# Gated linear attention with one routed token: spinning on zeros at the start, a router argmax in two levels, four q features inside the end of K, and the last attention tile turned by DMA

## The chip, the cores and the metric

The kernel runs on one core of a Trainium2 chip, in one launch. The metric is the device time of an execution in microseconds (us), the median of several runs. TensorE is called PE here, its weight loads PEld, VectorE DVE, ScalarE ACT, GpSimd POOL and SyncE SP, as in the profile. "Lnn" is line nn of the kernel before; where a line of the changed kernel is meant, the text says so.

## The reference

Three results are mixed: a linear attention `a`, a layer `b` that changes a single token, and a gate `g` per token.

```
x = A_x                                             # (1, 2048, 1024), bf16
g = sigmoid((x * gate_w).sum(-1))                   # one gate per token
q, k, v = split(x @ wqkv)                           # 32 heads of 32
phi(u) = concat(softmax(u @ w_phi), softmax(-(u @ w_phi)))   # 64 features per head
kv = sum_s phi(k)_s v_s ;  z = sum_s phi(k)_s
a = (phi(q) @ kv / (phi(q) @ z + 1e-6)) @ wo
r = x @ w_r ;  idx = argmax(r)                      # one token out of 2048
y = (silu(x[idx] @ w_gate) * (x[idx] @ w_up)) @ w_down * sigmoid(r[idx])
b = x, with y added to row idx                      # w_gate, w_up: 1024 x 3584
out = g * a + (1 - g) * b
```

## The kernel before, in words

A scheduler puts the program's instructions in order on each engine and sets the semaphores; the order in the code and the buffers of the pools decide what it can do. Each engine then works through its own list in that order. The 2048 tokens are 16 tiles of 128. There are three stages.

**V (to about 74 us).** Four tiles of x are loaded (`xs_t`, L247) and transposed on PE (`xT_tile`, L269, copied by DVE, L270); the other twelve come by transposing DMAs (L273), all issued on SP. `k_v` (L392) multiplies each tile with the value weights in three pieces of 256, 384 and 386 columns; the last two columns are the router's and the gate's weight rows, put there by `rows_in` (L260). `fold` (L287) multiplies the key and query weights with `w_phi` once, so that keys and queries give features directly; it needs sixteen transposed weight loads (`wT`, six buffers, L279).

**K (about 74 to 161 us).** 32 units: one tile and half the heads each. `k_s0` makes the feature inputs `pk` (L405, eight matmuls with 512 columns), ACT takes exp of plus and minus (`e`, L408 and L409, three buffers), DVE sums and inverts (`ssum` L412, `rs` L414), and the product `phi` (L417) is made on POOL, every fourth one on DVE. `k_kv` adds phi times v into PSUM (`kvps`, L426) five units later (`LAG`).

At the start of K stands the router, `gates_and_route` (L293). `r` is transposed to 16 rows of 128 (`rT`, L304), a DMA strings them into one row (`r_row`, L306), and DVE finds the maximum (L308) and its place (L310) among 2048 values on one partition. The place is read into registers of DVE and POOL, DVE copies the token's column out of `xT` (`xsT`, L313), and PE multiplies it with the gate's row (`gw_sel`, L315). A short chain over ACT, DVE and PE (`ee`, `cc`, `c_bc`) makes one factor of it.

The chosen token's layer runs beside K and Q in 21 chunks of 1 MB of weights (`ffn_chunk`, L352 and L369; pool `ring` with two buffers): each chunk is 32 narrow matmuls with `xsT` or, for `w_down`, with `hh`.

**Q (about 161 to 304 us).** `kv_finish` copies the sums out of PSUM into `KV` (L446, L448, L449), DVE and ACT in turns. Then one loop runs over 32 steps and some more: `q_front` (L463) makes 512 tokens of features for four heads, ACT writes their exponentials to `E` (L465, L466); four steps later `q_num` (L484) multiplies with KV, DVE scales (`T`, L492), POOL adds and divides (`U` L501, `o_sb` L502); a transposing DMA turns the tile (`oT`, L511), ACT scales x (`xg`, L521, four buffers), and `q_wo` multiplies with `wo` (`po`, L530) in two groups of eight matmuls per tile, some steps later (`WL`). DVE mixes (`o_out`, L533) and SP stores (L539). The last tile is not turned by a DMA but by eight transposes on PE (`oT_ps`, L515) and an ACT copy. At the end POOL adds `y` into the chosen row (L384), behind all stores.

PSUM pools matter for order: `psA` (two buffers) serves pv, pk and pq; `psB` (two) serves pT, pW, po and `oT_ps`; `psK` has one buffer for kvps or num; everything small, the router's products among them, shares one tile, `small_ps`.

Of the kernel before, what the change touches and what calls it, by code (L numbers as in the profile page):

```python
# [20 lines left out]
D = 1024  # L21
H = 32
DH = 32
NT = S // P
KB = D // P
# [4 lines left out]
NU = NT * 2  # L30
# [7 lines left out]
VW = 1026  # L38
TX = 4
# [126 lines left out]
def kernel(  # L166
# [14 lines left out]
    ring = main.enter_context(tc.tile_pool(name="ring", bufs=2))  # L181
# [9 lines left out]
    wk = kscope.enter_context(tc.tile_pool(name="wk", bufs=3))  # L191

# [48 lines left out]

    xtiles = {}
# [7 lines left out]
    wv_sb = wraw.tile([P, KB, VW], BF, name="wv_sb", tag="w16")  # L250
# [42 lines left out]
    def gates_and_route():  # L293
# [11 lines left out]
        r_row = const.tile([1, S], BF, name="r_row")  # L305
        nc.sync.dma_start(out=r_row[0:1, :], in_=rT[:])  # L306
        mx8 = const.tile([1, 8], F32, name="mx8")
        nc.vector.max(out=mx8[:], in_=r_row[:])  # L308
        ix8 = const.tile([1, 8], U32, name="ix8")
        nc.vector.max_index(out=ix8[:], in_max=mx8[:], in_values=r_row[:])  # L310
        idx_dve = nc.values_load(ix8[0:1, 0:1], engines=[ET.DVE], min_val=0, max_val=S - 1)
        moe["idx_pool"] = nc.values_load(ix8[0:1, 0:1], engines=[ET.Pool], min_val=0, max_val=S - 1)
# [5 lines left out]
        nc.scalar.activation(out=ee[:, 0:1], in_=mx8[0:1, 0:1], func=ACTF.Exp, scale=-1.0)  # L318
# [138 lines left out]
    def q_front(sb, j):  # L457
        if j == 0:
            est[sb] = qp["eb"].tile([P, KB, 2, SB], BF, name="E", tag="E")
        E = est[sb]  # L460
        pq = psA.tile([P, SB], F32, name="pq", tag="pA")
        for kb in range(KB):
            nc.tensor.matmul(pq[:], lhsT=wqf[:, kb, j * P:(j + 1) * P], rhs=xT[:, kb, sb * SB:(sb + 1) * SB],  # L463
                             start=(kb == 0), stop=(kb == KB - 1))
        nc.scalar.activation(out=E[:, j, 0, :], in_=pq[:], func=ACTF.Exp)  # L465
        nc.scalar.activation(out=E[:, j, 1, :], in_=pq[:], func=ACTF.Exp, scale=-1.0)  # L466

    def q_num(t, hf):
# [3 lines left out]
        if hf == 0:  # L472
            st = {"o": qw.tile([P, H, DH], BF, name="o_sb", tag="o_sb", bufs=5)}
            xin = qw.tile([P, D], BF, name="xin", tag="xin", bufs=8)
# [30 lines left out]
    def q_oT(t):  # L505
# [4 lines left out]
        if t < NT - 1:  # L510
            nc.sync.dma_start_transpose(out=oT[:], in_=o_f)  # L511
        else:
            oT_ps = psB.tile([P, KB, P], BF, name="oT_ps", tag="pB")
            for kb in range(KB):
                nc.tensor.transpose(out=oT_ps[:, kb, :], in_=o_f[:, kb * P:(kb + 1) * P], identity=ident[:])  # L515
            nc.scalar.copy(out=oT[:], in_=oT_ps[:])
# [31 lines left out]

    xT_tile(0)
    rows_in()  # L550
    k_v(0, 0)
# [36 lines left out]
    qp["eb"] = main.enter_context(tc.tile_pool(name="eb", bufs=2))  # L588
# [4 lines left out]
    WL = 6  # L593
    wq_ = []
    i = 0
    while i < n_front + NL + 2 or wq_:
# [11 lines left out]
        if i < n_front:  # L608
            q_front(i // KB, i % KB)
# [43 lines left out]
```

## Time and profile before

| what | before |
|---|---|
| median of 3 runs | 306.57 us (305.55 to 307.3) |
| the profiled execution's own time | 305.89 us |
| its span, first to last instruction | 304.2 us |
| granted TensorE clock, mean | 0.990 |
| PE busy | 278.5 us, 2483 matmuls |
| DVE busy | 185.0 us |
| ACT busy | 145.4 us |
| POOL busy | 126.1 us |
| DMA | 47.45 MB, 156 GB/s on average |

The profile shows one execution. A row of a timeline reads: start, duration, engine, line, operation, written tile, read tiles, shapes, how many were merged, and in brackets the idle time of the engine before the first with what ended it. A row of the waits reads: who waits, for whom, us in total, how often, the longest. A row of the windows gives a stretch, then for each engine the busy time and the count, then the granted clock, the share of DMA time and GB/s.

### The profile page before, as it was taken

What the parts mean: (1) busy time and instruction counts of PE and PEld (TensorE: products, weight loads), DVE (VectorE), ACT (ScalarE), POOL (GpSimd) and SP (SyncE); (2) the same over time, 40 slices, a digit from 0 to 9 for tenths busy, and PEclk for the clock granted to TensorE, in tenths of its full rate; (3) what the DMA queues carried; (4) which work ended last, traced back from release to release, by engine and by line L of the source; (5) the groups of instructions that cost most, each with busy time, mean ns of one, the idle gap of its engine ahead of it and who ended that gap; (6) DMA issues with size and microseconds to landing.
All of it is one profiled execution on the core that took longest, in us unless ns stands there. A gap on an engine that the chain in (4) does not pass through costs nothing. (4 is left out here: it accounts for less than half of the span.)

```text
span 304.2 us, 6228 instructions
## 1 busy us (share of the span) xinstructions
PE 278.5 (92%) x2483; PEld 163.7 (54%) x2518; DVE 185.0 (61%) x362; ACT 145.4 (48%) x266; POOL 126.1 (41%) x105
## 2 busy tenths in 40 slices
PE   2999999999898799999979999999999999996990
PEld 2756667766345456656545556555555555552440
DVE  3200015466899777778794677777668666694340
ACT  1133345877744343544427999465555443422100
POOL 6000000000166555755560588865556666674001
PEclk9999999999999999999999999999999999997998
DMA  7999999960001897766745989814542242134220
GB/s 205 283 178 186 197 336 294 150 122 0 1 2 29 269 313 240 260 203 213 254 168 183 313 326 258 168 38 104 131 111 71 52 106 69 34 94 98 69 87 25
DMA packets 76529, 47.45 MB, mean 156 GB/s; under 512 B 47824, under 2 KB 69328, under 8 KB 76496
## 3 DMA queue, kind: packets, MB, share of 16 engines
q1 hardware_dynamic: 75344, 46.94, 57.8%
q8 instruction: 21, 0.34, 0.5%
q10 hardware_dynamic: 1120, 0.07, 0.3%
q14 instruction: 12, 0.10, 0.1%
q0 software_dynamic: 32, 0.00, 0.0%
HBM read 31.53 MB, written 4.20 MB: 117 GB/s over the span
## 5 line engine op out<-in xcount | busy, mean ns | idle before, releaser
L417 POOL TENSOR_TENSOR phi<-e,rs 128x1024 bf16<-128x1024 bf16 x24 | 45.7, 1912 | 106.1 <-DVE rs L414 97.8
L405 PE MATMUL pk<-wkf,xT 128*128 128x512 bf16 x240 | 59.9, 379 | 2.9 <-ACT e L409 1.9
L530 PE MATMUL po<-wo_sb,oT 128*128 128x512 bf16 x249 | 59.7, 384 | 2.3 <-DVE o_out L533 1.7
L392 PE MATMUL pv<-wv_sb,xT 128*128 128x256 bf16 (+2 forms) x384 | 61.1, 313 | 0.3 <-DVE xT L270 0.3
L463 PE MATMUL pq<-xT,wqf 128*128 128x512 bf16 x244 | 60.5, 379 | 0.8 <-ACT E L466 0.2
L501 POOL TENSOR_TENSOR U<-T 128x512 f32<-128x512 f32 x32 | 40.6, 1268 | 43.1 <-DVE T L492 27.0
L392 PEld LDWEIGHTS <-xT 128*128 128x128 bf16 x384 | 37.1, 99 | 18.3 <-DVE xT L270 0.5
L412 DVE TENSOR_REDUCE ssum<-e 128x32 f32<-128x1024 bf16 x32 | 38.6, 1211 | 11.8 <-ACT e L409 11.8
L533 DVE SCALAR_TENSOR_TENSOR o_out<-po,gate,xg 128x512 bf16<-128x512 f32 x32 | 24.0, 750 | 32.1 <-PE po L530 32.0
L530 PEld LDWEIGHTS <-oT 128*128 128x128 bf16 x256 | 25.1, 99 | 31.0 <-issue 3.0
L408 ACT ACTIVATE e<-pk 128x512 bf16<-128x512 f32 x32 | 19.1, 597 | 41.6 <-PE pk L405 26.7
L492 DVE TENSOR_TENSOR T<-num,rS 128x1024 f32<-128x1024 f32 x32 | 38.9, 1215 | 0.0
L394 ACT CAST v_all<-pv 128x384 bf16<-128x384 f32 (+1 forms) x48 | 21.2, 444 | 34.7 <-PE pv L392 34.4
L405 PEld LDWEIGHTS <-xT 128*128 128x128 bf16 x256 | 22.8, 97 | 24.0 <-issue 2.3
L463 PEld LDWEIGHTS <-wqf 128*128 128x128 bf16 x256 | 23.4, 98 | 21.8 <-issue 0.3
L502 POOL TENSOR_TENSOR o_sb<-U,rden 128x512 bf16<-128x512 f32 x32 | 33.6, 1049 | 2.5
L521 ACT ACTIVATE xg<-xin,omg 128x1024 f32<-128x1024 bf16 x16 | 18.4, 1151 | 23.4 <-DVE o_out L533 23.4
L465 ACT ACTIVATE E<-pq 128x512 bf16<-128x512 f32 x32 | 19.1, 596 | 19.5 <-PE pq L463 19.3
L519 ACT ACTIVATE junk<-xin 128x1024 bf16<-128x1024 bf16 x16 | 17.0, 1062 | 11.6 <-DMA xin<-in_A_x_dram 11.5
L484 PEld LDWEIGHTS <-E 128*128 128x128 bf16 x256 | 17.0, 98 | 9.0 <-DVE T L492 2.6
L484 PE MATMUL num<-KV,E 128*128 128x136 bf16 x256 | 20.8, 223 | 0.2 <-DVE KV L449 0.2
L466 ACT ACTIVATE E<-pq 128x512 bf16<-128x512 f32 x32 | 19.0, 595 | 0.0
(95 smaller groups left out, 243.6 us busy)
## 6 DMA issues: line engine op xcount, KB each, us to landing
wch<-in_B_w_gate_dram SPq DMA_DIRECT2D x7, 1024.0 KB, 6.7
wch<-in_B_w_up_dram SPq DMA_DIRECT2D x7, 1024.0 KB, 5.1
wchd<-in_B_w_down_dram SPq DMA_DIRECT2D x7, 1024.0 KB, 5.8
xin<-in_A_x_dram SPq DMA_DIRECT2D x16, 256.0 KB, 4.1
out_dram<-o_out SPq DMA_DIRECT2D x32, 128.0 KB, 1.8
wo_sb<-in_A_wo_dram SPq DMA_DIRECT2D x1, 2048.0 KB, 13.8
wv_sb<-in_A_wqkv_dram SPq DMA_DIRECT2D x2, 768.0 KB, 8.2
xs_t<-in_A_x_dram SPq DMA_DIRECT2D x4, 256.0 KB, 4.5
```

The costliest lines, as they stand in the source:

```text
L392: nc.tensor.matmul(pv[:, 0:hi - lo], lhsT=xT[:, kb, t * P:(t + 1) * P], rhs=wv_sb[:, kb, lo:hi], start=(kb == 0), stop=(kb == KB - 1))
L394: nc.scalar.copy(out=v_all[:, t, h0:h1, 0:DH], in_=pv[:, 0:(h1 - h0) * DH].rearrange("p (h d) -> p h d", d=DH))
L405: nc.tensor.matmul(pkf, lhsT=xT[:, kb, t * P:(t + 1) * P], rhs=wkf[:, kb, hf * 512:(hf + 1) * 512], start=(kb == 0), stop=(kb == KB - 1))
L412: nc.vector.tensor_reduce(out=ssum[:], in_=e2, axis=AX.X, op=ALU.add)
L417: eng.tensor_tensor(out=phi[:].rearrange("p h s f -> p (h s) f"), in0=e2, in1=_bc(rs[:], [P, HH * 2, DH]), op=ALU.mult)
L463: nc.tensor.matmul(pq[:], lhsT=wqf[:, kb, j * P:(j + 1) * P], rhs=xT[:, kb, sb * SB:(sb + 1) * SB], start=(kb == 0), stop=(kb == KB - 1))
L484: nc.tensor.matmul(num[:, b * NSTR:b * NSTR + KVW], lhsT=E[:, j, sg, tl * P:(tl + 1) * P], rhs=KV[:, sg, j, :], start=True, stop=True)
L492: nc.vector.tensor_tensor(out=T[:].rearrange("p s (j h) d -> p (s j) h d", h=4), in0=nb[:, :, 0:128].rearrange("p b (h d) -> p b h d", d=D ...
L501: nc.gpsimd.tensor_tensor(out=U[:], in0=T[:, 0], in1=T[:, 1], op=ALU.add)
L502: nc.gpsimd.tensor_tensor(out=st["o"][:, hf * HH:(hf + 1) * HH, :], in0=U[:], in1=_bc(rden[:], [P, HH, DH]), op=ALU.mult)
L530: nc.tensor.matmul(po[:], lhsT=st["oT"][:, kb, :], rhs=wo_sb[:, kb, sl], start=(kb == 0), stop=(kb == KB - 1))
L533: nc.vector.scalar_tensor_tensor(out=o_out[:], in0=po[:], scalar=gate[:, t:t + 1], in1=st["xg"][:, sl], op0=ALU.mult, op1=ALU.add)
```

## The change

Five edits stand together.

1. A tile of zeros, `wz`, is written as DVE's first work. Seven 512-wide matmuls on it are issued before everything else on PE, and three more after `rows_in` in the code. They write `small_ps`, which nobody reads then.
2. The argmax goes in two levels. DVE finds the maximum and its place in each of the 16 rows of `rT`, adds the row's offset (`row0`, an iota on POOL), and a DMA brings the 16 pairs to one partition (`mrow`). There DVE takes the largest value, puts a large number on the place of every row that is below it (`cnd`), takes the smallest place (`ixf`) and casts it (`ixi`).
3. The pool `ring` of weight chunks has three buffers. The room of `wv_sb` (`w16`) becomes a pool of its own that `E` uses in turn with one buffer of `eb`; `xin` has seven buffers in place of eight.
4. The first four `q_front` (`NPRE`) are called inside the last steps of the K loop.
5. The last tile is turned by a transposing DMA like the others, and `WL` is 8 in place of 6, so that each `q_wo` comes two steps later.

```diff
+NPRE = 4
-    ring = main.enter_context(tc.tile_pool(name="ring", bufs=2))
+    w16 = main.enter_context(tc.tile_pool(name="w16", bufs=1))
+    ring = main.enter_context(tc.tile_pool(name="ring", bufs=3))
...
+    wz = const.tile([P, 512], BF, name="wz")
+    nc.vector.memset(wz[:], 0.0)
+
+    def spin(n):
+        for _ in range(n):
+            nc.tensor.matmul(small_ps[:, 0:512], lhsT=wz[:, 0:P], rhs=wz[:], start=True, stop=True)
...
+    nc.gpsimd.iota(row0[:], pattern=[[0, 1]], base=0, channel_multiplier=P, allow_small_or_imprecise_dtypes=True)
...
-        nc.sync.dma_start(out=r_row[0:1, :], in_=rT[:])
-        mx8 = const.tile([1, 8], F32, name="mx8")
-        nc.vector.max(out=mx8[:], in_=r_row[:])
-        nc.vector.max_index(out=ix8[:], in_max=mx8[:], in_values=r_row[:])
-        idx_dve = nc.values_load(ix8[0:1, 0:1], engines=[ET.DVE], min_val=0, max_val=S - 1)
+        nc.vector.max(out=mx8[:], in_=rT[:])
+        nc.vector.max_index(out=ix8[:], in_max=mx8[:], in_values=rT[:])
+        nc.vector.tensor_copy(out=mi[:, 0:1], in_=mx8[:, 0:1])
+        nc.vector.tensor_copy(out=mi[:, 1:2], in_=ix8[:, 0:1])
+        nc.vector.tensor_tensor(out=mi[:, 1:2], in0=mi[:, 1:2], in1=row0[:], op=ALU.add)
+        nc.sync.dma_start(out=mrow[0:1, :, :], in_=mi[:])
+        nc.vector.tensor_reduce(out=mxv[:], in_=mrow[:, :, 0], axis=AX.X, op=ALU.max)
+        nc.vector.tensor_scalar(out=cnd[:], in0=mrow[:, :, 0], scalar1=mxv[:, 0:1], scalar2=float(2 * S),
+                                op0=ALU.is_lt, op1=ALU.mult)
+        nc.vector.tensor_tensor(out=cnd[:], in0=cnd[:], in1=mrow[:, :, 1], op=ALU.add)
+        nc.vector.tensor_reduce(out=ixf[:], in_=cnd[:], axis=AX.X, op=ALU.min)
+        nc.vector.tensor_copy(out=ixi[:], in_=ixf[:])
+        idx_dve = nc.values_load(ixi[0:1, 0:1], engines=[ET.DVE], min_val=0, max_val=S - 1)
...
-            est[sb] = qp["eb"].tile([P, KB, 2, SB], BF, name="E", tag="E")
+            ep = w16 if sb % 2 == 0 else qp["eb"]
+            est[sb] = ep.tile([P, KB, 2, SB], BF, name="E", tag="w16" if sb % 2 == 0 else "E")
...
-        if t < NT - 1:
-            nc.sync.dma_start_transpose(out=oT[:], in_=o_f)
-        else:
-            oT_ps = psB.tile([P, KB, P], BF, name="oT_ps", tag="pB")
-            for kb in range(KB):
-                nc.tensor.transpose(out=oT_ps[:, kb, :], in_=o_f[:, kb * P:(kb + 1) * P], identity=ident[:])
-            nc.scalar.copy(out=oT[:], in_=oT_ps[:])
+        nc.sync.dma_start_transpose(out=oT[:], in_=o_f)
...
+    spin(7)
     xT_tile(0)
     rows_in()
+    spin(3)
     k_v(0, 0)
...
+        if i >= NU and i - NU < NPRE:
+            q_front(0, i - NU)
...
-    WL = 6
+    WL = 8
...
-        if i < n_front:
+        if NPRE <= i < n_front:
             q_front(i // KB, i % KB)
```

What that does to the order shows best at three places. The first is DVE at the start of K, where `ssum` and `rs` belong to the K units and the rest to the router. Before:

```order
L412 TENSOR_REDUCE ssum<-e 128x32 x2
L414 RECIPROCAL rs<-ssum 128x32 x2
L412 TENSOR_REDUCE ssum<-e 128x32
L308 MAX mx_961<-r_row 1x8
L414 RECIPROCAL rs<-ssum 128x32
L310 MAX_INDEX ix_963<-mx_961,r_row 1x8
L412 TENSOR_REDUCE ssum<-e 128x32
L311 TENSOR_LOAD ix_963
...
L313 COPY xsT<-xT 128x8
```

The same place in the changed kernel (its lines), from the arrival of the 16 pairs on:

```order
L437 TENSOR_REDUCE ssum<-e 128x32 x2
L327 TENSOR_REDUCE mxv<-mrow 1x1
L439 RECIPROCAL rs<-ssum 128x32
L329 TENSOR_SCALAR cnd<-mrow,mxv 1x16
L439 RECIPROCAL rs<-ssum 128x32
L331 TENSOR_TENSOR cnd<-cnd,mrow 1x16
L437 TENSOR_REDUCE ssum<-e 128x32
L333 TENSOR_REDUCE ixf<-cnd 1x1
L439 RECIPROCAL rs<-ssum 128x32
L335 CAST ixi<-ixf 1x1
L336 TENSOR_LOAD ixi
...
L338 COPY xsT<-xT 128x8
```

The merge lies between the sums of the first three units, and no sum stands between the cast and the register load any more, as one did between L310 and L311.

The second place is PE at the start of K. The numbers tell buffers apart; each row stands for a run of like matmuls and their weight loads. Before:

```order
L405 MATMUL pk_1076<-wkf_112,xT_109 128x512
...
L426 MATMUL kvps_126<-v_all_113,phi_1020 128x66
...
L405 MATMUL pk_1136<-wkf_112,xT_109 128x512
...
L426 MATMUL kvps_126<-v_all_113,phi_1038 128x66
...
L405 MATMUL pk_1162<-wkf_112,xT_109 128x512
...
L426 MATMUL kvps_126<-v_all_113,phi_1056 128x66
...
L405 MATMUL pk_1222<-wkf_112,xT_109 128x512
...
L315 MATMUL small_ps_125<-gw_sel_122,xsT_121 1x1
```

And in the changed kernel, from the same fifth pk tile on:

```order
L430 MATMUL pk_1106<-wkf_117,xT_114 128x512
...
L340 MATMUL small_ps_130<-gw_sel_127,xsT_126 1x1
...
L451 MATMUL kvps_131<-v_all_118,phi_1050 128x66
...
L430 MATMUL pk_1166<-wkf_117,xT_114 128x512
...
L451 MATMUL kvps_131<-v_all_118,phi_1068 128x66
...
L430 MATMUL pk_1192<-wkf_117,xT_114 128x512
L349 MATMUL small_ps_130<-cc_1029,ones_row_101 128x1
```

The product of `gw_sel` with `xsT`, which stood behind three kv groups and most of three pk tiles, now stands directly behind the fifth pk tile.

The third place is the end of PE's list, behind the last num. Before:

```order
L530 MATMUL po_4042<-wo_sb_111,oT_3673 128x512
...
L515 MATMUL oT_ps_4055<-ident_91,o_sb_3852 128x128
...
L334 MATMUL small_ps_125<-nbb_4072,ones_col_98 1x2
...
L530 MATMUL po_4081<-wo_sb_111,oT_3727 128x512
...
L515 MATMUL oT_ps_4055<-ident_91,o_sb_3852 128x128
...
L530 MATMUL po_4081<-wo_sb_111,oT_3727 128x512
```

In the changed kernel:

```order
L550 MATMUL po_4048<-wo_sb_116,oT_3628 128x512
...
L359 MATMUL small_ps_130<-nbb_4069,ones_col_103 1x2
...
L550 MATMUL po_4078<-wo_sb_116,oT_3679 128x512
...
L550 MATMUL po_4090<-wo_sb_116,oT_3679 128x512
...
L550 MATMUL po_4102<-wo_sb_116,oT_3733 128x512
```

The eight transposes are gone. Of the 256 po matmuls 98 stand behind the last num, where before it was 82. Further up, 32 pq matmuls have moved in among the last five kv groups of K, and between the last kv group and the first num of Q stand 96 chunk and 19 pq matmuls, where before it was 64 and 21.

More of the change, by code (lines that the diff above doesn't have):

```diff
@@ L240, in kv_slot @@
         return kvps[:, pr * KSTR:pr * KSTR + 66]
+    row0 = const.tile([NT, 1], F32, name="row0")
+    nc.gpsimd.iota(row0[:], pattern=[[0, 1]], base=0, channel_multiplier=P, allow_small_or_imprecise_dtypes=True)
     xtiles = {}
@@ L248, in xload @@
         xtiles[t] = xt_
-    wv_sb = wraw.tile([P, KB, VW], BF, name="wv_sb", tag="w16")
+    wv_sb = w16.tile([P, KB, VW], BF, name="wv_sb", tag="w16")
     xload(0)
@@ L473, in q_num @@
             st = {"o": qw.tile([P, H, DH], BF, name="o_sb", tag="o_sb", bufs=5)}
-            xin = qw.tile([P, D], BF, name="xin", tag="xin", bufs=8)
+            xin = qw.tile([P, D], BF, name="xin", tag="xin", bufs=7)
             nc.sync.dma_start(out=xin[:], in_=x2[t * P:(t + 1) * P, :])
```

16 lines of the change are left out of this document (11 added, 5 removed).

## The prediction

> **What bounds the kernel now.** I read the page's busy times first, then the waits of TensorE (PE), then the windows and timelines around each wait.
>
> ```profile
> PE 278.5 (92%) x2483; PEld 163.7 (54%) x2518; DVE 185.0 (61%) x362; ACT 145.4 (48%) x266; POOL 126.1 (41%) x105
> ...
> PE pT L269 <- DMA xs_t<-in_A_x_dram: 5.5, 2, 3.8
> PE small_ps L356 <- DMA wch<-in_B_w_gate_dram: 2.1, 2, 1.8
> PE pk L405 <- ACT e L409: 1.9, 3, 1.0
> PE po L530 <- DVE o_out L533: 1.7, 1, 1.7
> PE kvps L426 <- POOL phi L417: 1.5, 1, 1.5
> PE kvps L426 <- DVE phi L417: 1.3, 2, 0.8
> ```
>
> PE is the bound: 278.5 of the 304.2 us span. The rest is the start, the end after the last matmul, and the waits above, which come at stage borders. The change must win there, or where PE runs on half its clock.
>
> ```profile
> 40.00:60.00 20.00, 20.00 (x170) 13.92 (x169) 9.01 (x18) 12.84 (x28) 0.00 (x0) 1.00 1.09 263
> 80.00:100.00 20.00, 18.02 (x185) 9.93 (x187) 19.07 (x27) 8.91 (x19) 11.39 (x6) 1.00 0.11 33
> ...
> 277.80:281.10 3.30, 3.08 (x11) 1.21 (x11) 0.87 (x2) 1.01 (x1) 0.00 (x0) 0.50 0.01 3
> ...
> 285.00:297.00 12.00, 11.25 (x52) 4.91 (x51) 5.23 (x8) 0.00 (x0) 0.00 (x0) 1.00 0.23 78
> ```
>
> After the times come busy us (and count) of PE, PEld, DVE, ACT, POOL, then the granted clock. In the V stage (40 to 60) PE never waits. At the start of K (80 to 100) it idles 1.98 us, and DVE is full (19.07 of 20). From 277.8 to 281.1 the clock is 0.50. The last row gives the full-clock pace of 512-wide matmuls: 11.25 / 52 = 0.216 us.
>
> **The start.**
>
> ```profile
> 5.62 0.33 SPq L247 DMA_DIRECT2D xs_t<-in_A_x_dram  x1
> ...
> xs_t<-in_A_x_dram SPq DMA_DIRECT2D x1, 256.0 KB, 6.1
> ...
> 6.85 1.04 PE L269 MATMUL pT<-ident,xs_t 128*128 128x128 bf16 x8 [1.67 <-DMA xs_t<-in_A_x_dram]
> 7.68 3.62 PE L392 MATMUL pv<-wv_sb,xT 128*128 128x256 bf16 x16
> 11.09 1.30 PE L269 MATMUL pT<-ident,xs_t 128*128 128x128 bf16 x16
> 12.68 0.50 PE L392 MATMUL pv<-wv_sb,xT 128*128 128x256 bf16 x3 [0.29 <-DVE xT L270]
> 13.24 0.93 PE L392 MATMUL pv<-wv_sb,xT 128*128 128x256 bf16 x7
> ```
>
> Sixteen matmuls start between 7.68 and 11.09: 0.213 us each. Later seven take 0.93, about 0.11 each once the last one's latency is off. So PE is on half clock until about 11. The eight transposes at 6.85 take 0.83 until the next matmul; at full clock 0.43. The change spins seven 512-wide matmuls before the first transposes (3.0 us at half clock, estimated at twice 0.216 each; the memset of `wz` is DVE's first work, so they run from about 1.3 to 4.3. That pushes the transposes at 3.79 back by 0.5, which the 1.67 of waiting before 6.85 hides; without that wait it would cost the 0.5) and three more before the second value matmul. If PE is fast from 6.85, it would be through the 16 by 6.85 + 0.43 + 0.65 + 1.73 = 9.7. But then the fourth x tile is late: issued at 5.62, it lands 6.1 us later, at 11.7. Its transposes end near 12.2, where 12.68 stood: **-0.5**, not the 2 us that the clock alone suggests. If PE is still slow, three spins of 0.43 sit on the path, partly taken up by the wait at 11.7: +0.4 to +0.8.
>
> The Trainium skill ("TensorE: Matmul & The Clock Gate", Part 1) says that full clock comes after one busy window of 3413 ns, and that the windows run free of the kernel. By it, 3 us of spin followed by a gap wakes PE only in some executions, and the sum below would be about 1 us higher in the others.
>
> **The router at the start of K.** The argmax over 2,048 values on one partition becomes 16 rows of 128, then a merge of 16 pairs.
>
> ```profile
> 79.78 5.34 PE L405 MATMUL pk<-wkf,xT 128*128 128x512 bf16 x23 [1.04 <-ACT e L409]
> 82.03 0.55 DVE L414 RECIPROCAL rs<-ssum 128x32 f32<-128x32 f32 x2
> 82.55 3.78 POOL L417 TENSOR_TENSOR phi<-e,rs 128x1024 bf16<-128x1024 bf16 x2 [76.43 <-DVE rs L414]
> 83.96 2.27 DVE L308 MAX8 mx<-r_row 1x8 f32<-1x2048 bf16 x1
> 86.44 2.27 DVE L310 FIND_INDEX8 ix<-mx,r_row 1x8 uint32<-1x2048 bf16 x1
> 90.05 0.17 DVE L313 COPY xsT<-xT 128x8 bf16 x1 [0.23 <-DVE ssum L412]
> 90.45 0.34 PE L315 MATMUL small_ps<-gw_sel,xsT 128*1 128x1 bf16 x8
> ...
> r_row<-rT SPq DMA_DIRECT2D x1, 4.0 KB, 1.8
> ```
>
> Two DVE passes of 2.27 go: 4.5 us off DVE. About ten small operations of 0.1 to 0.3 come (like the 0.17 and 0.09 of `xsT` and, below, `cc`); POOL's iota is done long before. The new DMA (`mrow`) is issued near 79.6 and, taking 1.8 like `r_row`, lands at 81.4, before DVE is free at 82.1. But the order also moves the eight `gw_sel` matmuls: they stand right behind the fifth pk tile, ahead of every kv matmul. PE gets there at 79.78 + 5.34 = 85.1 and stops until `xsT` is there. Queued behind the stop are kv group 0, whose phi is ready at 84.5, and the next pk tile; ACT's exponentials wait for that tile, and DVE's sums for them. So the index now has a due time, 85, where before PE had 5.4 us more of other work ahead of it (`gw_sel` at 90.45).
>
> When does it come? From the index to `xsT` the register load takes 90.05 - 88.71 = 1.34 us; before, a reduction covered it, now nothing does. And the merge falls into POOL's phi products, 82.55 to 88.5. These rows show what DVE does beside POOL:
>
> ```profile
> 92.99 0.09 DVE L323 TENSOR_TENSOR cc<-ee 1x1 bf16<-1x1 f32 x1
> ...
> 153.65 1.91 POOL L417 TENSOR_TENSOR phi<-e,rs 128x1024 bf16<-128x1024 bf16 x1 [0.28 <-ACT sg L360]
> 154.63 0.96 DVE L361 TENSOR_SCALAR sg<-sg 128x28 f32<-128x28 f32 x1
> ...
> 275.21 1.27 POOL L501 TENSOR_TENSOR U<-T 128x512 f32<-128x512 f32 x1 [0.23 <-DVE T L492]
> 276.28 0.21 DVE L340 TENSOR_TENSOR bb<-bb 1x1 f32<-1x1 f32 x1
> ```
>
> 28 elements take 0.96 us and end at 155.59, just behind POOL's 155.56. One element takes 0.21 and ends at 276.49, just behind POOL's 276.48; with POOL idle its like took 0.09. So some DVE operations wait out POOL's. Before, the two long passes ran beside POOL at full speed, and the rest of the chain met an idle POOL. In the new chain the add of `cnd` and `mrow` (two SBUF inputs, as L340) is such a one. I work it through: rs ends 82.45, phi(0) holds until 84.6, add 84.7, reduction of 1.2 to 85.9, minimum, rs and cast to 86.6, register 1.34, `xsT` 88.0 to 88.6, `gw_sel` near **88.6**. PE idles 3.5, then 0.4 more for `cc`, against the 1.9 that go: +2.1. A stop that long should also halve the clock, as the row at 277.80 shows after a stretch with 1.73 and 0.70 of waits: 3.4 us at half clock is 1.7, less the 0.4 then hidden: +1.3. Together **+3.4**. Bounds: nothing blocked, `gw_sel` at 86.4, -0.6; a second phi before the add, `gw_sel` at 90.6, +5.8.
>
> The Trainium skill ("SBUF — State Buffer", Who interferes with whom) says that copies and casts within SBUF can need the same port pair. No row here shows the cast or the `xsT` copy under POOL; by the page `gw_sel` is at 88.9 and the sum 0.3 higher.
>
> **The weight chunks.**
>
> ```profile
> 103.68 0.95 PE L356 MATMUL small_ps<-xsT,wch 128*128 128x1 bf16 x32 [1.79 <-DMA wch<-in_B_w_gate_dram]
> ```
>
> The third chunk was late by 1.79, a later one by 0.3. With three buffers it is loaded before K: **-2.1** (from -1.5). Its megabyte now goes ahead of `wo_sb` and ten key weight loads: 4 us at the 263 GB/s of the row at 40. PE does not wait there now, so part of 4 us may show; with the smaller drifts of the Q stage (`WL` 8, 7 `xin` buffers) I take **+0.4** (0 to +1.5).
>
> **From K to Q.**
>
> ```profile
> 157.98 0.43 PE L426 MATMUL kvps<-v_all,phi 128*128 128x66 bf16 x8 [1.51 <-POOL phi L417]
> ...
> 160.79 0.43 PE L426 MATMUL kvps<-v_all,phi 128*128 128x66 bf16 x8 [0.43 <-DVE phi L417]
> ...
> 167.51 0.35 PE L484 MATMUL num<-KV,E 128*128 128x136 bf16 x3 [0.16 <-DVE KV L449]
> ```
>
> Four q tiles (4 x 1.73 us, eight matmuls each) now lie between the last five kv groups; the last phi is there long before. 1.51 + 0.43 go, and about the 0.16. The tiles' exponentials (E) go into the room of `wv_sb`, which the V stage has long left, so ACT need not wait for the K stage's memory; eight of them stand before the KV casts in ACT's order, but the last is done within 1.2 us of its tile, about when the last kv ends. Next late is KV: 6.3 us from the last kv to its last copy (161.2 to 167.5). PE then has 96 chunk matmuls (three chunks at 0.9) and 19 q matmuls (4.1): 6.8 us, which covers it. **-2.0** (from -1.2).
>
> **The tail.**
>
> ```profile
> 273.22 0.59 PE L530 MATMUL po<-wo_sb,oT 128*128 128x512 bf16 x2
> ...
> 275.94 1.02 PE L530 MATMUL po<-wo_sb,oT 128*128 128x512 bf16 x4 [1.73 <-DVE o_out L533]
> 277.66 0.58 PE L515 MATMUL oT_ps<-ident,o_sb 128*128 128x128 bf16 x4 [0.70 <-POOL o_sb L502]
> 280.09 16.21 PE L530 MATMUL po<-wo_sb,oT 128*128 128x512 bf16 x71
> ...
> 275.14 0.74 DVE L533 SCALAR_TENSOR_TENSOR o_out<-po,gate,xg 128x512 bf16<-128x512 f32 x1
> ```
>
> Behind the last num stand 82 po matmuls: 17.7 us at 0.216, 18.4 with the few small ones. They took 273.22 to 296.30, 23.1: 4.7 lost to the waits, to eight transposes and to half clock. `oT_ps` held one of the two psB buffers that po needs. Now 98 po follow without transposes (16 of them were done earlier before, so no PE work is added). One wait stays: the second group after the last num needs the buffer that the `o_out` at 275.14 frees at 275.9, and PE is there at 275.4 (273.65 and one group of 1.73), so about 0.6 with the start. The last tile is turned by a DMA on SP's queue, with only output stores behind it; its product is the last of the 12 groups, 19 us later, so its few us are hidden. Were that cover gone, they would be bare. No wait is left that could halve the clock. **-4.1** (-3.3 to -4.7).
>
> **Sum.** -0.5 + 3.4 - 2.1 + 0.4 - 2.0 - 4.1 = -4.9. The profiled execution took 305.89 us (span 304.2 and 1.7 around it): **301.0**. It lies 0.7 under the median of 306.57; from that the sum gives 301.7.
>
> **Rivals.**
> - The router is quick: no blocking, `gw_sel` at 86.4, -0.6 for +3.4: 297.0. For it: POOL's start trails rs by 0.2. Against it: L340.
> - POOL's second phi goes ahead of the waiting add: 90.6, +5.8: 303.4. No row shows who goes first when both wait.
> - The spin does not wake PE (+0.8 for -0.5): 302.3.
> - Slower: four operations of the chain (`cnd`, add, cast, `xsT`) each wait out a phi of 1.91. `gw_sel` at 93.3: a stop of 8.2 for 1.9, and two halved stretches of 1.7: +9.8, in all 307.4. It decides from `gw_sel` at about 92. Against it: only three phi are ready then.
>
> **How the numbers follow.** Forecast 0.45, quick router 0.24, second phi 0.17, no waking 0.07, slower 0.07. The range 296.2 to 304.0 takes in the first four with their bounds and leaves half of the quick cases' lower tail and the slower case out. A measurement tells about 0.5% (1.5 us): faster 0.89, within 0.07, slower 0.04.
>
> **What would show it.** Right: at the start, a PE wait for the fourth x tile's DMA ahead of its transposes, near 10 to 11.7; PE waiting for DVE `xsT` for 3 to 4 us near 85, with a 0.50 clock behind it; the add of `cnd` as long as what is left of POOL's phi; no wait on `wch`; no wait on phi at the end of K; some 98 po after the last num with one wait. Wrong: `gw_sel` after a wait of under 2 us (the quick router), a half clock after the spins' end (no waking), waits of the folds on `wT`, or po waits in the tail of more than 1 us.

## The result, and the profile after

| | before | changed |
|---|---|---|
| time, median of 4 runs | 306.94 us (305.55 to 308.44) | 296.65 us (295.86 to 297.04) |
| ratio | | 0.966, 95% interval 0.961 to 0.971 |
| profiled execution | 305.89 us, span 304.2 | 297.04 us, span 295.3 |

The changed kernel is 3.4% faster. The forecast was 301.0 with a range of 296.2 to 304.0: the sign is right, the time lies just inside, and the point is 4.3 us too high. By the medians the change is worth 10.3 us (8.9 between the two profiled executions), twice the 4.9 of the forecast. It came out where the quick-router rival (297.0) had put it. Ratios, here and below, leave disturbed runs out; medians and ranges are of all runs.

The first part of the page and the PE waits of the changed kernel, to be laid beside those of before:

```profile
PE 278.5 (94%) x2487; PEld 162.6 (55%) x2520; DVE 181.9 (62%) x371; ACT 143.5 (49%) x265; POOL 126.1 (43%) x106
...
PE pT L280 <- DMA xs_t<-in_A_x_dram: 2.1, 2, 1.2
PE small_ps L340 <- DVE xsT L338: 1.4, 1, 1.4
PE small_ps L200 <- DVE wz L196: 1.3, 1, 1.3
PE pk L430 <- ACT e L434: 1.0, 1, 1.0
PE small_ps L271 <- DMA rows<-in_gate_w_dram: 0.7, 1, 0.7
PE small_ps L349 <- DVE cc L348: 0.4, 1, 0.4
```

PE is busy 278.5 us in both, ten spins among them now; the 8.9 us came out of its idle time and its half clock. The waits for `wch`, for the last phi and for `o_out` are gone. New are the stop for `xsT`, 1.35 us, and 0.42 for `cc`. That is the first surprise: the forecast had a stop of 3.5 there, with a half clock behind it.

Where the time came from, by the two traces: the first pk starts at 74.74 instead of 73.90 (+0.84). From there to the end of the last po it took 222.40 us before (73.90 to 296.30) and 212.47 after (74.74 to 287.21): -9.93. What follows the last po grew by 0.16.

PE's timeline at the start, and the clock in two of its windows (time, busy us and count of PE, PEld, DVE, ACT, POOL, then the granted clock):

```profile
1.35 3.15 PE L200 MATMUL small_ps<-wz 128*128 128x512 bf16 x7 [1.35 <-DVE wz L196]
4.31 0.64 PE L280 MATMUL pT<-ident,xs_t 128*128 128x128 bf16 x8
5.61 0.16 PE L271 MATMUL small_ps<-ident,rows 16*128 16x16 bf16 x1 [0.67 <-DMA rows<-in_gate_w_dram]
6.94 0.62 PE L280 MATMUL pT<-ident,xs_t 128*128 128x128 bf16 x8 [1.16 <-DMA xs_t<-in_A_x_dram]
...
8.52 3.10 PE L417 MATMUL pv<-wv_sb,xT 128*128 128x256 bf16 x15
...
12.98 0.62 PE L280 MATMUL pT<-ident,xs_t 128*128 128x128 bf16 x8 [0.92 <-DMA xs_t<-in_A_x_dram]
```
```profile
7.76:11.17 3.41, 3.41 (x16) 2.06 (x15) 0.53 (x1) 0.38 (x1) 0.00 (x0) 0.50 1.05 346
4.35:7.76 3.41, 1.58 (x21) 1.21 (x20) 1.10 (x4) 1.06 (x1) 1.67 (x10) 1.00 1.11 241
```

The spins did wake PE: from 4.35 on the clock is 1.00. But in the next 3.41 us PE had only 1.58 us of work, since it waited for the rows and for the second x tile, and from 7.76 to 11.17 it stood at 0.50 again, just when the value matmuls came. The fourth x tile's transposes start at 12.98, when the tile lands.

DVE's timeline at the merge, with POOL's phi beside it:

```profile
82.94 0.33 DVE L439 RECIPROCAL rs<-ssum 128x32 f32<-128x32 f32 x1
83.20 0.12 DVE L329 TENSOR_SCALAR cnd<-mrow,mxv 1x16 f32<-1x16 f32 x1
83.25 0.33 DVE L439 RECIPROCAL rs<-ssum 128x32 f32<-128x32 f32 x1
83.51 0.10 DVE L331 TENSOR_TENSOR cnd<-cnd,mrow 1x16 f32<-1x16 f32 x1
...
86.64 0.62 DVE L338 COPY xsT<-xT 128x8 bf16 x1 [1.37 <-issue]
...
88.31 0.81 DVE L345 TENSOR_SCALAR ee<-ee 1x2 f32<-1x2 f32 x1
```
```profile
83.45 5.65 POOL L442 TENSOR_TENSOR phi<-e,rs 128x1024 bf16<-128x1024 bf16 x3 [77.32 <-DVE cnd L329]
```

The add of `cnd` and `mrow` begins 0.06 behind the first phi and takes 0.10: not held. The copy of `xsT` takes 0.62 (0.17 before) and the TENSOR_SCALAR of `ee` 0.81; they end at 87.26 and 89.12, the second and the third phi at 87.23 and 89.10. So those two were held. The Trainium skill ("SBUF — State Buffer", Who interferes with whom) says that copies can need the port pair that GpSimd uses; the 0.62 agrees.

The tail:

```profile
265.34 0.59 PE L550 MATMUL po<-wo_sb,oT 128*128 128x512 bf16 x2
...
266.04 6.28 PE L550 MATMUL po<-wo_sb,oT 128*128 128x512 bf16 x26
```

The two-group stretch that held 1.73 and 0.70 us of waits, eight transposes and a half clock is now an unbroken row of po.

### The profile page after: what moved, and what is told of

The parts are those of the page before. It is cut to its first block, busy times and chain, and to the rows that moved or that the text cites. A ratio compares the mean times of both kernels' runs of the same rounds, so it can differ in the third digit from the quotient of the medians.

```text
span 295.3 us, 6251 instructions
## 1 busy us (share of the span) xinstructions
PE 278.5 (94%) x2487; PEld 162.6 (55%) x2520; DVE 181.9 (62%) x371; ACT 143.5 (49%) x265; POOL 126.1 (43%) x106
## 5 line engine op out<-in xcount | busy, mean ns | idle before, releaser
L550 PE MATMUL po<-wo_sb,oT 128*128 128x512 bf16 x248 | 58.8, 379 | 0.5
```

The costliest lines, as they stand in the source:

```text
L550: nc.tensor.matmul(po[:], lhsT=st["oT"][:, kb, :], rhs=wo_sb[:, kb, sl], start=(kb == 0), stop=(kb == KB - 1))
```

## The experiments

Each variant is the changed kernel with one edit; two of them (`cc` later too, tiles on ACT's queue) carry an edit of another variant besides. The medians are of 6 runs each (4 for the changed kernel, which was timed in the first session alone), and the ratio is to the kernel before in the same session. Since the kernel before itself came out between 305.05 and 306.94 in the four sessions that ran it more than once, two medians of different sessions tell apart about 1 us and no less. So the table has a second measure that leaves the start out: the time in the trace from the start of the first pk to the end of the last po.

| variant | median us (range) | ratio, 95% interval | first pk to last po |
|---|---|---|---|
| changed | 296.65 (295.86 to 297.04) | 0.966 (0.961 to 0.971) | 74.74 to 287.21 = 212.47 |
| no spins | 296.43 (295.79 to 297.18) | 0.969 (0.964 to 0.974) | 73.80 to 286.94 = 213.14 |
| 16 spins | 297.24 (296.32 to 299.93) | 0.972 (0.967 to 0.978) | 75.60 to 288.01 = 212.41 |
| one-level argmax | 297.67 (296.64 to 299.12) | 0.972 (0.968 to 0.977) | 75.00 to 289.14 = 214.14 |
| `gw_sel` one unit later | 297.17 (296.63 to 299.23) | 0.973 (0.968 to 0.978) | 74.02 to 286.72 = 212.70 |
| no q tiles in K | 299.48 (298.34 to 303.40) | 0.978 (0.973 to 0.982) | 74.28 to 289.13 = 214.85 |
| two chunk buffers | 303.00 (299.90 to 305.02) | 0.985 (0.979 to 0.990) | 75.51 to 295.02 = 219.51 |
| last tile turned on PE | 300.13 (299.29 to 301.56) | 0.980 (0.976 to 0.984) | 75.73 to 291.26 = 215.53 |
| WL = 6 | 297.31 (295.46 to 299.13) | 0.971 (0.966 to 0.976) | 74.64 to 287.56 = 212.92 |
| `cc` later too | 295.84 (294.79 to 297.06) | 0.967 (0.962 to 0.972) | 73.98 to 286.05 = 212.07 |
| tiles on ACT's queue | 297.73 (296.09 to 299.52) | 0.974 (0.968 to 0.980) | 75.73 to 287.97 = 212.24 |

### The start: no spins, sixteen spins, tiles on another queue

```diff
-    spin(7)
+    spin(0)
...
-    spin(3)
+    spin(0)
```

> The changed kernel without its ten spins; everything else stands in the same order. Theory (the start is set by the landing of the fourth x tile, 12.94 us, and the spins only woke the clock for one window of 3.4 us, from 4.35 to 7.76, which ended before the value matmuls could use it): the first pk comes within 0.3 us of the 74.74 of the changed kernel if that tile lands as late as there, and 0.8 earlier if it lands at 11.7 as in the kernel before; the time is 0 to 0.8 us below the changed kernel's 296.65, so 295.8 to 296.7. Rival (the spins do help, as the sum on record had it, -0.5): the time is 0.5 us or more above it, 297.2 or later.

Without spins, and the rest of every engine's list unchanged, PE's timeline reads:

```profile
12.04 0.62 PE L280 MATMUL pT<-ident,xs_t 128*128 128x128 bf16 x8 [0.26 <-DMA xs_t<-in_A_x_dram]
...
73.80 0.81 PE L430 MATMUL pk<-wkf,xT 128*128 128x512 bf16 x3
```

The fourth tile's transposes start at 12.04, the first pk at 73.80: 61.76 later. In the changed kernel it is 74.74 - 12.98 = 61.76 too. The time, 296.43, is 0.2 from the changed kernel's. The theory holds: within what these runs tell apart the spins neither cost nor gain, and the 0.84 by which K starts later in the changed kernel's trace is the later landing of one tile. Whether the spins have a part in when that tile lands is open: it landed between 11.45 and 13.20 in the eleven traces with spins that keep the queues as they are, at 11.73 and 11.99 in the two without.

```diff
-    spin(7)
+    spin(16)
...
-    spin(3)
+    spin(0)
```

> Sixteen spins in one piece ahead of the first transposes (7 and 3 before), so that PE has no idle stretch between waking and the first value matmuls. The spins end near 6.5 (8 at half clock, 8 at full). Theory (the tile's landing sets the start): the granted clock stays at 1.0 from about 4.4, the sixteen value matmuls are through near 9.8, and PE then waits 2 to 3 us for the fourth x tile instead of 0.9; of the half-clock time only the value matmuls left behind that landing are saved, at most 0.9 us: 295.8 to 296.6, and up to 0.8 above 296.65 if the wait puts the clock back to a half. Rival (the clock alone sets the start): the first pk comes 1.7 us earlier, and the time is near 294.9.

```profile
7.81 1.92 PE L417 MATMUL pv<-wv_sb,xT 128*128 128x256 bf16 x16
...
12.64 0.62 PE L280 MATMUL pT<-ident,xs_t 128*128 128x128 bf16 x8 [2.47 <-DMA xs_t<-in_A_x_dram]
```

Now the sixteen value matmuls run at full clock, 1.92 us instead of the 4.2 that they took in the changed kernel with three spins among them, and PE waits 2.47 instead of 0.92 for the tile. The first pk came at 75.60, 62.96 behind the transposes, because this execution also had a wait of 1.2 for a folded weight (`wT`), one of the drifts that the forecast had listed. No gain in any case: what the clock gives, the tile's wait takes.

```diff
-        nc.sync.dma_start(out=xt_[:], in_=x2[t * P:(t + 1) * P, :])
+        (nc.scalar if t in (2, 3) else nc.sync).dma_start(out=xt_[:], in_=x2[t * P:(t + 1) * P, :])
```

(The small loads of `BDm` on ACT's queue go behind the x tiles for it, and the 16 spins stay.)

> The changed kernel with the third and fourth x tiles issued on ACT's queue, behind the two row loads and ahead of three of the four loads of BDm, and with 16 spins in one piece as in the run before. Theory (the fourth tile's landing alone sets the start, since the first pk came 61.8 us behind it in the changed kernel and in four of its variants): the tile is issued near 2.5 in place of 5.9, lands 2 to 3 us earlier, and with the clock awake PE follows: the first pk 1 to 2 us earlier, 294.7 to 295.7. Rival (the bytes ahead set it, x tiles and value weights together): the value weights' second part lands that much later, PE waits for it in place of the tile, and the time stays within 0.4 of 296.65.

```profile
9.26 0.62 PE L280 MATMUL pT<-ident,xs_t 128*128 128x128 bf16 x8 [1.84 <-DMA xs_t<-in_A_x_dram]
...
11.55 1.05 PE L280 MATMUL pT<-ident,xs_t 128*128 128x128 bf16 x16
```

The third and the fourth tile are there when PE wants them (16 transposes in one piece), but now the second is late: its transposes start at 9.26 instead of 6.94. The first pk came at 75.73, 1.52 of it a wait for `wT`. The time, 297.73, is above both forecasts. The rival was nearer, with another place for the wait: with the third and the fourth tile issued ahead, the second landed at 9.21 instead of 6.89.

### The router: one level again, and the matmuls later

```diff
-        mx8 = const.tile([NT, 8], F32, name="mx8")
-        nc.vector.max(out=mx8[:], in_=rT[:])
...
+        r_row = w16.tile([P, KB * VW], BF, name="r_row", tag="w16")[0:1, 0:S]
+        nc.sync.dma_start(out=r_row, in_=rT[:])
+        mx8 = const.tile([1, 8], F32, name="mx8")
+        nc.vector.max(out=mx8[:], in_=r_row)
...
```

> The changed kernel with the router's argmax in one level again (two passes over 2,048 values on one partition); the rest as changed, but gw_sel stands again behind three kv groups, as in the kernel before. If the two levels cost what the prediction on record says (+3.4), the time falls to about 293.3. If they are worth what the two traces say when laid side by side (-0.3, the stop for xsT being 1.35 us and without a half clock behind it), the time is 0 to 1 us above 296.65: 296.6 to 297.6.

The time did not fall by 3.4; at 297.67 it is 1 us above the changed kernel's, which these runs can't tell from no difference. In the trace PE's idle time from the first to the last pk is 2.75 us, and 2.81 in the run without spins, which has the two-level router and no missing record: the two routers stop PE equally long, at other places (0.82 for a phi and 0.64 for an e here). The 1.67 by which this trace is longer in the table is a half clock, which the windows show:

```profile
93.49:96.90 3.41, 2.36 (x21) 1.37 (x22) 3.41 (x10) 1.73 (x4) 1.91 (x1) 1.00 0.00 0
96.90:100.32 3.42, 3.42 (x110) 2.95 (x108) 2.96 (x4) 1.53 (x3) 3.40 (x2) 1.00 0.35 81
100.32:103.73 3.41, 3.41 (x16) 1.49 (x15) 3.23 (x4) 1.09 (x2) 0.57 (x2) 0.50 1.09 386
```

```diff
-    gates_and_route()
+    route = gates_and_route(); next(route)
...
+        if i in (5, 6): next(route)
```

(The function yields ahead of `gw_sel` and ahead of the matmul of `cc`.)

> The two-level router as changed, but the eight gw_sel matmuls are issued one K unit later (behind one kv group and one pk tile) and the matmul of cc behind them one more. Theory (the stop is only due to gw_sel standing too early in PE's order): the waits of 1.35 for xsT and 0.42 for cc go, 1.3 to 1.8 us: 294.9 to 295.4. Rival (PE at the start of K is held by ACT and DVE anyway, DVE is busy 4.78 of 5 us from 80 to 85): a wait for e or phi takes the stop's place and the time stays within 0.4 of 296.65.

The time, 297.17, is not below the changed kernel's. The 1.35 for `xsT` went, and in the waits stood `PE small_ps L349 <- DVE cc L348: 1.7` in its place, with 1.4 for pk instead of 1.0: no gain. The stop had only moved on to the next step of the same chain. So `cc` was moved as well:

```diff
+        if i in (5, 10): next(route)
```

> As the run with gw_sel one K unit later, but the matmul of cc four units later still (c_bc is only read by the last gate step, 13 chunks later). Theory (PE only lost at the places where the router stands in its order): no wait for xsT and none for cc, 1.7 us less than the changed kernel: 294.7 to 295.4. Rival (DVE, busy 4.78 of 5 us at that place, holds PE by e or phi whatever the router does): waits of pk for e or of kvps for phi add up to the same 1.8, and the time stays at 296.3 to 297.2.

```profile
PE pk L430 <- ACT e L434: 1.4, 2, 1.0
...
PE small_ps L381 <- DVE small_ps L351: 0.6, 1, 0.6
```

Both router waits are gone, 1.77 us. 0.4 for e and 0.6 for a memset that stands behind `cc` came instead, so 0.8 should be left; from the first pk to the last po it is 0.4 less, and the median is 0.8 lower, between the theory's range and the rival's. It has the lowest median of all, but by its ratio (0.967, 0.962 to 0.972) it is not to be told from the changed kernel.

### The lock

Seven small operations on DVE, with nobody using their results, behind each phi that POOL makes:

```diff
+        if 8 <= u < 31 and eng is nc.gpsimd:
+            pf, pb, pu = probes
+            a, b, eb = rs[0:1, 0:16], rs[0:1, 16:32], e2[0:1, 0, 0:16]
+            for k in range(4):
+                kind = (u * 4 + k) % 7
+                if kind == 0:
+                    nc.vector.tensor_tensor(out=pf[:, 0:16], in0=a, in1=b, op=ALU.add)
...
```

> The changed kernel with small extra operations on DVE in the K stage, 16 elements each on one partition, behind the product of every unit whose phi POOL makes (their results are used by nobody): an add of two f32 inputs, a TENSOR_SCALAR on f32, a copy of f32, a copy of bf16, a cast of f32 to integer, an add of two bf16 inputs and a reduction of f32. An operation that stands beside a running POOL phi (1.9 us) and takes about 0.1 us is free; one that ends just behind phi's end was held. The prediction on record (two SBUF inputs are held): both adds end with phi, the others take 0.1. Theory from the changed kernel's trace (its f32 add of 0.10 and its cast of 0.08 were free, TENSOR_SCALAR of 0.81 and the bf16 copy of 0.62 were held): the f32 add, the cast and the reduction are free, TENSOR_SCALAR and the copies are held. Third view (the add only slipped through because phi had begun 0.06 us before it): all but the reduction are held in the middle of a phi. The time matters little here.

Two places of DVE's timeline in that run, the router's own add and one of the probes, and POOL's phi beside each:

```profile
82.56 0.10 DVE L331 TENSOR_TENSOR cnd<-cnd,mrow 1x16 f32<-1x16 f32 x1
...
108.29 0.15 DVE L454 TENSOR_SCALAR pf<-rs 1x16 f32<-1x16 f32 x1
108.39 1.88 DVE L452 TENSOR_TENSOR pf<-rs 1x16 f32<-1x16 f32 x1
```
```profile
82.51 1.91 POOL L443 TENSOR_TENSOR phi<-e,rs 128x1024 bf16<-128x1024 bf16 x1 [76.37 <-DVE cnd L329]
...
108.34 1.91 POOL L443 TENSOR_TENSOR phi<-e,rs 128x1024 bf16<-128x1024 bf16 x1 [1.85 <-DVE rs L440]
```

The probe's add of 16 elements at 108.39 takes 1.88 us and ends 0.02 behind phi. That falls on the side of the forecast: an add of two SBUF inputs is held. So are the TENSOR_SCALAR, both copies, the cast and the bf16 add where they stand in a phi; a reduction is free (0.15). My theory that the f32 add is free falls. Of the third view the outcome stands (all but the reduction were held), but not its reason: in this one run the router's add begins 0.05 into its phi and is through in 0.10, while three probe adds that begin 0.05 to 0.06 into theirs are held for 1.88, and other held operations begin from 0.02 on. The start on record does not tell the two apart. The kernel took 316.97 us in its one run, 20 more than the changed one, for 72 operations that take 0.1 to 0.2 each when free.

To see whether the form of the router's add (its second input at every second element) had saved it, its forms were tried behind two reductions, well inside phi:

```diff
+                if kind == 0:
+                    nc.vector.tensor_tensor(out=pf[0:1, 0:16], in0=a, in1=c2, op=ALU.add)
...
+                elif kind == 2:
+                    nc.vector.tensor_copy(out=pf[0:1, 0:1].bitcast(U32), in_=a[:, 0:1])
...
```

> The changed kernel with other small extra operations on DVE in the K stage, behind two reductions, so that several stand in the middle of a phi: the forms of the router's own chain, which were free beside phi in the changed kernel though the f32 add of the run before was held 1.80 to 1.88 us from only 0.05 us into phi on. They are the add with its second input read at every second element, as mrow is, the cast of one element, as ixi, the TENSOR_SCALAR and the copy that read every second element, as cnd, the strided bf16 copy of 128x8, as xsT, the add of one element, and as a control the add of the run before. Theory (the form decides: what reads or writes in single elements or steps does not wait): the strided add and the cast of one element take 0.05 to 0.2 us in the middle of a phi, the control ends 0.02 us behind phi's end. Rival (the place decides: two earlier operations of the chain had luck): the strided add and the cast of one element are held to phi's end like the control.

DVE's and POOL's timelines at two places of it:

```profile
105.55 0.14 DVE L460 CAST pf<-rs 1x1 uint32<-1x1 f32 x1
105.72 1.29 DVE L462 TENSOR_TENSOR pf<-rs 1x1 f32<-1x1 f32 x1
...
151.32 1.46 DVE L456 TENSOR_TENSOR pf<-rs,st 1x16 f32<-1x16 f32 x1
```
```profile
105.10 1.91 POOL L445 TENSOR_TENSOR phi<-e,rs 128x1024 bf16<-128x1024 bf16 x1 [0.46 <-DVE pf L460]
...
150.85 1.91 POOL L445 TENSOR_TENSOR phi<-e,rs 128x1024 bf16<-128x1024 bf16 x1 [0.45 <-PE pk L433]
```

The strided add is held (1.46, to 152.78, phi to 152.76), and so is the add of one element. The cast of one element is not (0.14 at 105.55, 0.45 into phi). So for `ixi`'s cast the form decided; for the router's add the form alone is no reason, since the strided add is held in the middle of a phi. In all twelve traces of the two-level router that add begins 0.05 to 0.06 into phi's record and takes 0.10: the same program gets it through every time. Operations of a held form that began 0.45 to 1.71 into a phi were held every time here, 16 of 16, and in the run before so were the 15 that began 0.02 to 0.18 into one. What let the router's add through is therefore open. One difference on record is the operation ahead of it: a reciprocal of 0.33 us that began 0.21 ahead of phi, where ahead of the three held probe adds stood a TENSOR_SCALAR of 0.15 that began 0.05 ahead of it. Whether that decides was not tried.

### The chunk buffers

```diff
-    ring = main.enter_context(tc.tile_pool(name="ring", bufs=3))
+    ring = main.enter_context(tc.tile_pool(name="ring", bufs=2))
```

> The changed kernel with two weight-chunk buffers instead of three. Theory (the third chunk's transfer can only start when the first is used, at 92 to 94, and takes longer than PE needs to get to it): a PE wait of about 1.8 us for wch comes back, 298.2 to 299.1; up to 1.7 more if this wait puts the clock to a half. Rival (the chunks would be in time, since the stop for xsT holds PE anyway): within 0.6 of 296.65.

Slower by 3.3 us in the fastest of its runs (299.90 against 296.65) and by 6.3 in the median: more than the forecast's 2.1, and not for its reason. The wait for the third chunk in K does not come back: it is 0.26 where it was 1.79. That chunk landed 5.44 us after its issue here and 6.96 after it in the trace of before, so most of the 1.79 was one late landing. The waits stand in the Q stage, in PE's, ACT's and SP's timelines of the profiled execution, which was the slowest one:

```profile
171.78 0.38 PE L398 MATMUL small_ps<-hh,wchd 128*128 128x1 bf16 x9 [1.81 <-DMA wchd<-in_B_w_down_dram]
...
197.89 0.81 PE L489 MATMUL pq<-xT,wqf 128*128 128x512 bf16 x3 [1.93 <-ACT E L492]
```
```profile
194.53 1.06 ACT L539 ACTIVATE junk<-xin 128x1024 bf16<-128x1024 bf16 x1 [2.69 <-DMA xin<-in_A_x_dram]
```
```profile
183.29 0.38 SPq L394 DMA_DIRECT2D wchd<-in_B_w_down_dram  x1
188.87 1.27 SPq L536 DMA_TRANSPOSE oT<-o_sb  x1
190.19 1.05 SPq L501 DMA_DIRECT2D xin<-in_A_x_dram  x2
```

PE waits at 197.89 for an exponential; the exponential stands on ACT behind a square of `xin`; `xin` was issued only at 190.19, on SP's queue behind a chunk load that waited for its buffer until 183.29 and behind a transposing DMA that went out at 188.87. With three buffers the same two loads, the seventh and eighth of `xin`, were issued at 173.0 and 173.6. How much of the six microseconds is this chain, how much the wait of 1.81 for a `w_down` chunk, and how much the half clock from 172.54 to 175.95, one trace cannot say. At least 3.3 us is in all six runs, but only the slowest was traced, so that the faster ones lose their 3.3 us at the same places is not shown.

### The q tiles in K

```diff
-NPRE = 4
+NPRE = 0
```

> The changed kernel without the four q tiles inside the end of K (NPRE = 0). The prediction on record has them at -2.0 us, the two traces laid side by side at about -2.5; if so, the last kv groups wait for phi again (1.5 and 0.4 us in the kernel before) and the time is 298.3 to 299.4. Rival (what the tiles hide was hidden by other work already, the chunk matmuls having moved with the third buffer): within 0.6 of 296.65.

```profile
155.60 0.43 PE L451 MATMUL kvps<-v_all,phi 128*128 128x66 bf16 x8 [1.52 <-POOL phi L442]
...
158.41 0.43 PE L451 MATMUL kvps<-v_all,phi 128*128 128x66 bf16 x8 [0.22 <-DVE phi L442]
...
165.16 0.35 PE L510 MATMUL num<-KV,E 128*128 128x136 bf16 x3 [0.19 <-DVE KV L474]
```

The three waits of before are back (1.51, 0.43 and 0.16 there), the first and the last almost to the digit, the second at half its size. The time is 299.48, 2.8 above the changed kernel and at the upper end of what was expected; by the table's traces it is 2.4.

### The tail

```diff
-        nc.sync.dma_start_transpose(out=oT[:], in_=o_f)
+        if t < NT - 1:
+            nc.sync.dma_start_transpose(out=oT[:], in_=o_f)
+        else:
+            oT_ps = psB.tile([P, KB, P], BF, name="oT_ps", tag="pB")
...
```

> The changed kernel with the last attention tile turned by eight PE transposes through oT_ps, as before; WL stays at 8. Theory (oT_ps holds one of the two buffers that po needs while it waits for the last o_sb, and the waits then put the clock to a half for 3.4 us): 3 to 4.7 us slower, 299.7 to 301.4, with a po wait of 1.7, an oT_ps wait of 0.7 and a clock of 0.50 in the tail. Rival (the 16 po that WL = 8 moves behind the last num cover the waits): within 1 us of 296.65.

```profile
268.88 1.02 PE L556 MATMUL po<-wo_sb,oT 128*128 128x512 bf16 x4 [1.73 <-DVE o_out L559]
270.61 0.40 PE L541 MATMUL oT_ps<-ident,o_sb 128*128 128x128 bf16 x4 [0.70 <-POOL o_sb L528]
```

300.13, 3.5 slower, with both waits of before at their old size (1.73 and 0.70). In this execution no half clock followed them, so the 3.06 in the table is the price without it.

```diff
-    WL = 8
+    WL = 6
```

> The changed kernel with WL = 6, so that 82 po stand behind the last num and not 98; the last tile is still turned by DMA. Theory (the turn by DMA alone makes the gain of the tail, and the 16 po only change their place): within 0.5 of 296.65. Rival (the gain needs the longer reserve): 1 us or more slower, with a wait of po for oT before the last groups.

297.31, 0.7 above, a little more than the theory's 0.5 but less than two medians tell apart; no wait of po for oT. The turn by DMA alone makes the tail's gain, as far as these runs can show.

## Why the prediction was right or wrong

**The router: +3.4 forecast, about 0 measured.** This step failed. The forecast put "the add of `cnd` and `mrow`" behind the start of the first phi and had it wait until 84.6. The rule it used is borne out by both sets of probes, and the add did begin behind phi's start, by 0.06; yet it was not held. The step took every start inside phi's record as held, and why this one got through stays open. Had it been held to phi's end, 85.37, all behind it would come 1.8 later (85.37 - 83.61) and the stop would be 3.1 instead of 1.35, close to the forecast's 3.5. The half clock of +1.3 fell with it: the poorest window of 3.41 us around the stop (86.26 to 89.67) still holds 2.36 us of PE work, and the clock stayed. The forecast knew the alternative as a rival with 0.24; a row of before from which phi's start could be had only to 0.2 us (POOL's start behind rs) was no ground for 0.45 against 0.24. With nothing for +3.4 the sum is -8.3, and the two profiled executions differ by 8.9. So the time lies in the stated range because the range took in that rival, not because the path behind 301.0 was right. Taking the stop away altogether gave about 0.8 us, and going back to one level cost 1.0, neither clear of the noise, so the router's edit is worth little either way. (A slip of 0.1 stands in the sum itself: 3.5 + 0.4 - 1.9 is 2.0.)

**The start: -0.5 forecast, nothing measured.** The limit was named rightly (the fourth tile's landing), and so was the caution: by the Trainium skill ("TensorE: Matmul & The Clock Gate", Part 1) the clock's windows run free of the kernel, and the traces agree: seven spins had woken PE by 4.35 in the changed kernel, but only by 10.69 in the run with `gw_sel` one unit later. What failed is first the premise that PE is fast from 6.85: in the changed kernel's trace it was at half clock again from 7.76 to 11.17. And the size failed: the tile landed at 11.45 to 13.20 and not always at the 11.7 of one trace, a spread larger than the whole term.

**The weight chunks: -2.1, and +0.4 for the drift.** The wait of 1.79 went, but not by the third buffer alone, as the term had it: with two buffers only 0.26 of it came back, for the chunk's transfer took 5.44 us there and 6.96 in the trace of before. Still, undoing the edit costs 3.3 us at least. The one trace of it shows where: a chunk wait of 1.81 and late `xin` loads, both in the Q stage. The term saw only the wait that stood in the trace of before, not the queue that the chunk loads share. The +0.4 did not show in the changed kernel; waits for `wT` of 1.2 and 1.5 stood in two of the twelve variants' traces.

**From K to Q: -2.0.** Right: -2.4 by the table, with the three waits that the forecast named.

**The tail: -4.1.** Right in mechanism: 3.5 by undoing the turn, and 3.06 in a trace without half clock. The one wait of 0.6 that the forecast left in the tail did not come.

The terms as undone one by one (router 1.0, chunks 6.3, tiles 2.8, turn 3.5, spins 0) add up to 13.6 by the medians, more than the 10.3 of the whole change. Each is a difference of medians of two sessions, good to about 1 us. That the edits also lean on each other (with the tiles inside K and the tail at full pace, the queue's delays in Q have less to hide behind) is likely, but no run undid two of them together.

## What to carry to other kernels

A small DVE operation beside a long GpSimd one took 0.1 us here or up to the whole 1.9 of the other, and its start in the trace did not tell which; so a chain of such operations on the critical path is costed with both ends open, or put where the other engine is idle. A stop taken from one step of a dependent chain shows up at the next step, so move the whole chain's consumers. A buffer more can be worth what its loads hold up in their queue, and the one wait that a trace shows for it may be a single late landing.

## What the runs showed of the hardware

The granted clock moves on a fixed grid: in each trace every change is a multiple of 3.413 us from every other, with another offset in each execution (4.35, 7.76, 11.17 and 291.07 in the changed kernel's, the last 82 steps on; 10.69 and 290.58 in that of `gw_sel` one unit later). The windows tell when it falls. Before the half-clock stretch of the changed kernel PE was busy 1.58 of 3.41 us (above); in the kernel that turns on PE, at the start:

```profile
8.91:12.32 3.41, 1.38 (x17) 1.11 (x14) 0.69 (x1) 0.75 (x2) 0.00 (x0) 1.00 1.08 338
12.32:15.73 3.41, 3.21 (x20) 2.48 (x21) 0.69 (x1) 0.38 (x1) 0.00 (x0) 0.50 1.34 169
```

There 1.38 us of work was followed by a half clock, in the two-buffer kernel 1.60 (169.13 to 172.54). In the kernel without q tiles in K it stayed full behind a window with 1.86:

```profile
152.38:155.79 3.41, 1.86 (x34) 1.14 (x33) 3.05 (x7) 1.08 (x2) 2.70 (x2) 1.00 0.84 297
155.79:159.20 3.41, 3.19 (x29) 1.52 (x26) 2.82 (x4) 1.08 (x2) 0.00 (x0) 1.00 0.02 4
```

So it did not take an idle window: half of one was enough, in windows that lie by chance. The waits of 1.73 and 0.70 in the tail were followed by 3.4 us at half clock in the trace of before, where all but 0.1 us of them fell into one window (274.31 to 277.72, 1.08 us of PE work), and by none in that of the kernel that turns on PE, where they were split between two (2.24 and 2.16). The Trainium skill ("TensorE: Matmul & The Clock Gate", Part 1) has a fall after an idle window of about 3.4 us, which the 1.38 to 1.60 us of work do not bear out. Busy time alone draws no border either: in the trace of before the clock stayed full behind a window with 1.51, all of it 512-wide po (294.79 to 298.20). And in the one-level router's trace a window with PE busy all 3.42 us (96.90 to 100.32) was followed by a half clock; 96 matmuls of one column took most of it. That busy time of such narrow matmuls counts for less is an explanation that was only argued, not tried.
